# Folding the score rows in two ahead of a top-32 selection, with GpSimd making the smaller halves and VectorE closing the gates

## Chip, cores and metric

One Trainium2 chip, one NeuronCore of it. The time is that of the device from the first to the last instruction of the slowest core (here the only one), in microseconds. The engines are TensorE (PE; PEld is its weight load), VectorE (DVE), ScalarE (ACT), GpSimd (POOL) and SyncE (SP), which issues the DMAs.

## What is computed

Attention that keeps, in each row of scores, only the 32 largest (and what ties with the 32nd), then a feed-forward layer with ELU. Eight batches, eight heads, 576 positions, head size 64; 4608 tokens of 512 go through 512 x 2048 and 2048 x 512 weights.

```python
scores = scale * np.matmul(q, k.transpose(0, 1, 3, 2))
kth = np.partition(scores, -top_k, axis=-1)[..., -top_k:-top_k + 1]   # top_k = 32
scores = np.where(scores >= kth, scores, -1000000000.0)
attn = np.exp(scores - np.max(scores, axis=-1, keepdims=True))
attn = attn / (np.sum(attn, axis=-1, keepdims=True) + 1e-09)
x = ...  # np.matmul(attn, v), heads side by side: 4608 x 512
h = x @ w_in
g = np.where(h > 0.0, h, np.exp(np.minimum(h, 0.0)) - 1.0)
out = g @ w_out
```

The weights arrive as 64-bit floats and are decoded to 32 bits by the kernel's first part.

## The kernel before

**Steps.** A step is one tile of 128 queries for two heads: two rows of 576 scores on each partition. There are 144, eighteen to a batch. The list `steps` fixes their order, and the loop at the end of the function writes the program for step n with work of four ages side by side: scores of step n+2, selection of step n, mask of step n-1 (`prev`), transposes of step n-2 (`done`). From step 8 on (`tight`) the order on PE, ACT, DVE and POOL is the order in which the code writes the instructions; nothing is moved afterwards. Each engine works its own list in that order and waits where an operand is not there.

**One step, in the order written.** `scores` (L331, copied out of PSUM by ACT at L339) for n+2; `attend` (L470) when a group of steps is turned; then the selection `select`, a generator that the loop advances four times, and between the pieces: `feed`; `mask(prev, 0)`; `feed`; `turn(done, main)` and `turn(done, rest)`; `mask(prev, 1)`; `feed`; `turn(done, other)`; `normalise(prev)`; `feed`.

- `select` (DVE): for each of the two rows MAX8 gives the eight largest, MATCH_REPLACE8 (with a load of the eight values) strikes them out, four rounds in all; L373, L378, L385. `u.first` keeps the first eight (the largest is the maximum), `u.last` the last eight (the last is the 32nd largest).
- `mask`: POOL takes the gap of 32nd and largest (L406); ACT makes a steep Prelu about the 32nd (L407), then the Exp with its sum (L408, with the gap as bias).
- `normalise` (POOL): five small operations for the reciprocal (L418 to L423), then each row times it (L425).
- `turn`: nine 128 x 128 transposes on PE (L444), copied to `et` by ACT (L445).
- `attend`: product with v on PE, ACT copies it into the block's `xT` (L497).

**The feed-forward beside it.** Tokens are gathered in blocks of one, two or three slots of 128. When the last head of a block is there, `ffn_pieces` appends its pieces: sixteen of `hidden` (four products each, L545) and four of `project` for each slot (L573). `feed`, four times a step, hands out as many pieces as the costs `HIDDEN` and `PROJECT` and the due times of the blocks allow. A unit of hidden is two pieces or more: ACT writes Relu(-h) to `n` (L555) and Relu(h) to `gT` (L558), then Exp of -n (L560). What is left, gT + n - 1, is the gate. It is put on the list `gates` and written by `close_gates` at a later feed (two feeds later, as a rule), or at the latest when a `project` needs it. Until some way past step 11, and for the last block, the gate is one operation on DVE (L517). For all others ACT first takes 1 from `n` (L564) and POOL adds (L515).

**Early steps.** Steps 0 to 7 select row by row (`select_row`) and share the engines with the decoding of the weights, in 37 pieces run by `hook`, at the end of rounds of the selection. When the list is empty, `hook` opens the pools that take the place of the raw weights (the dictionary `late`).

Of the kernel before, what the change touches and what calls it, by code (L numbers as in the profile page):

```python
# [7 lines left out]

AF = mybir.ActivationFunctionType
ALU = mybir.AluOpType  # L10
FP32 = mybir.dt.float32
U32 = mybir.dt.uint32
I32 = mybir.dt.int32
# [3 lines left out]
TOP_K = 32  # L17
TAKEN = -1.0e30
# [63 lines left out]
def kernel(  # L82
# [9 lines left out]
    nc = tc.nc  # L92
    P = nc.NUM_PARTITIONS
    B, H, S, D = q.shape
# [4 lines left out]
    HS = S // 2  # L99
# [4 lines left out]
    T = 3 * P  # L104
# [7 lines left out]
    def pool(name, bufs, **kw):  # L112
        return ctx.enter_context(tc.tile_pool(name=name, bufs=bufs, **kw))
# [4 lines left out]
    wkpool = pool("wk", 1)  # L118
    etpool = pool("et", 2)
    small = pool("small", 4)  # L120
# [2 lines left out]
    ps_sc = pool("ps_sc", 1, space=PSUM)  # L123
    ps_t = pool("ps_t", 2, space=PSUM)
    ps_f = pool("ps_f", 2, space=PSUM)
    wide = [ps_sc.tile([P, 2, JP], FP32, tag=f"s{i}", name="scps") for i in range(2)]
    late = {}
    raws = ExitStack()
# [70 lines left out]
    def hook():  # L199

        if not decode:
            return
        decode.pop(0)()
        if not decode:
            raws.close()
            late["f"] = ctx.enter_context(tc.tile_pool(name="f", bufs=2))
            late["g"] = ctx.enter_context(tc.tile_pool(name="g", bufs=2))
            late["x"] = ctx.enter_context(tc.tile_pool(name="xt", bufs=2))
            late["in"] = ctx.enter_context(tc.tile_pool(name="in", bufs=2))
# [134 lines left out]
    def select_row(u, i, decoding):  # L344
        if i == 0:
            u.first = small.tile([P, 2, 8], FP32, tag="m1", name="m1")
            u.last = small.tile([P, 2, 8], FP32, tag="m4", name="m4")
        sc = u.sc[:, i, :]
        m = u.first[:, i, :]
        nc.vector.max(m, sc)  # L350
        wk = wkpool.tile([P, S], FP32, tag=f"wk{i}", name="wk")
        cur = sc
        for r in range(TOP_K // 8 - 1):
            nc.vector.match_replace(wk[:], m, cur, TAKEN)
            cur = wk[:]
            if r < TOP_K // 8 - 2:
                m = small.tile([P, 8], FP32, tag=f"m{i}", name="m")[:]
            else:
                m = u.last[:, i, :]
            nc.vector.max(m, cur)  # L360
            if r > 0 and decoding:
                hook()
            if r != 1:
                yield

    def select(u):

        u.first = small.tile([P, 2, 8], FP32, tag="m1", name="m1")
        u.last = small.tile([P, 2, 8], FP32, tag="m4", name="m4")
        cur = [u.sc[:, i, :] for i in range(2)]  # L370
        found = [u.first[:, i, :] for i in range(2)]
        for i in range(2):
            nc.vector.max(found[i], cur[i])  # L373
        yield
        wk = [wkpool.tile([P, S], FP32, tag=f"wk{i}", name="wk")[:] for i in range(2)]
        for r in range(TOP_K // 8 - 1):
            for i in range(2):
                nc.vector.match_replace(wk[i], found[i], cur[i], TAKEN)  # L378
            cur = wk
            for i in range(2):  # L380
                if r < TOP_K // 8 - 2:
                    found[i] = small.tile([P, 8], FP32, tag=f"m{i}", name="m")[:]
                else:
                    found[i] = u.last[:, i, :]
                nc.vector.max(found[i], cur[i])  # L385
            hook()
            yield

    def mask(u, i, early=False):

# [111 lines left out]
    gates = []  # L502
    place = [0]

    def close_gates(keep=0, upto=None):

        while gates:
            put, group, dst, n, apart = gates[0]  # L510
            if put > place[0] - keep if upto is None else group > upto:
                return
            gates.pop(0)
            if apart:
                nc.gpsimd.tensor_tensor(dst, n, dst, ALU.add)  # L515
                continue
            nc.vector.scalar_tensor_tensor(  # L517
                out=dst, in0=n, scalar=-1.0, in1=dst, op0=ALU.add, op1=ALU.add
            )

    def ffn_pieces(blk):
        n_tok = blk.slots * P
        bank = dm // n_tok
        unit = max(2, bank)

        def hidden(f):
            if f == 0 and blk.number == 0:
                g = early.tile([P, NF, P], FP32, tag="g", name="gT")
                blk.gT = [g[:, 0:NG], g[:, NG:NF]]
            elif f % NG == 0 and blk.number > 0:  # L530
                g = late["g"].tile([P, NG, T], FP32, tag="g", name="gT")
                blk.gT.append(g[:])
            if f % unit == 0:
                if len(gates) > 1:
                    close_gates(upto=gates[0][1])
                if blk.number == 0:
                    n = earlyf.tile([P, 4 * P], FP32, tag="n", name="n")
                else:
                    n = late["f"].tile([P, 2 * T], FP32, tag="n", name="n")
                blk.n = n[:, 0 : unit * n_tok].rearrange("p (f t) -> p f t", f=unit)  # L540
            if f % bank == 0:
                ps = ps_f.tile([P, dm], FP32, tag="f", name="hps")
                blk.h = ps[:, 0 : bank * n_tok].rearrange("p (f t) -> p f t", f=bank)
            for i in range(NC):
                nc.tensor.matmul(  # L545
                    blk.h[:, f % bank, :],
                    w_in[:, i, f * P : (f + 1) * P],
                    blk.xT[:, i, 0:n_tok],
                    start=(i == 0),
                    stop=(i == NC - 1),  # L550
                )
            g, end = blk.gT[f // NG], f % NG + 1
            if end % bank == 0:
                n0 = f % unit + 1 - bank
                nc.scalar.activation(  # L555
                    blk.n[:, n0 : n0 + bank, :], blk.h, AF.Relu, scale=-1.0
                )
                nc.scalar.activation(g[:, end - bank : end, 0:n_tok], blk.h, AF.Relu)  # L558
            if end % unit == 0:
                nc.scalar.activation(blk.n, blk.n, AF.Exp, scale=-1.0)  # L560
                dst = g[:, end - unit : end, 0:n_tok]
                apart = place[0] > 4 * (tight + 3) and blk is not blocks[-1]
                if apart:
                    nc.scalar.activation(blk.n, blk.n, AF.Copy, bias=-1.0)  # L564
                gates.append((place[0], (blk.number, f + 1 - unit), dst, blk.n, apart))

        def project(s, part):
            close_gates(upto=(blk.number, (part + 1) * NF // 4 - 1))
            if part == 0:
                blk.o = ps_f.tile([P, dm], FP32, tag="f", name="ops")  # L570
            step = NF // 4
            for f in range(part * step, (part + 1) * step):
                nc.tensor.matmul(  # L573
                    blk.o[:],
                    blk.gT[f // NG][:, f % NG, s * P : (s + 1) * P],
                    w_out[:, f, :],
                    start=(f == 0),
                    stop=(f == NF - 1),
                )
            if part == 3:  # L580
                o = opool.tile([P, dm], FP32, tag="osb", name="osb")
                nc.scalar.copy(o[:], blk.o[:])
                for t in blk.tiles[s]:
                    p0 = t.cols.start - s * P
                    nc.sync.dma_start(out[t.rows, :], o[p0 : p0 + t.ql, :])

        part = HIDDEN[blk.slots]
        behind = 2 * NF if blk.number else 0
        return [
            (part, max(behind, NC * (f // 4 + 1)), lambda f=f: hidden(f))  # L590
            for f in range(NF)
        ] + [
            (PROJECT, max(behind, NF + (part + 1) * NF // 4),
             lambda s=s, part=part: project(s, part))
            for s in range(blk.slots)
            for part in range(4)
        ]
# [3 lines left out]
    blocks, tight = [], 2 * NHP  # L601
    for b in range(B):
        if b % 2 == 0:
            rest = 2 * J
# [4 lines left out]
            for part in division:  # L609
                blk = Block(len(blocks), len(part))  # L610
# [20 lines left out]
        for qts in order:  # L631
            for hp in range(NHP // 2 if qts == (J,) else NHP):
                group = Group([tiles[qt] for qt in qts], hp)
                steps += [Step(tiles[qt], hp, group, i) for i, qt in enumerate(qts)]
            for qt in qts:
                n = len(steps)
# [12 lines left out]
    for b in range(1, B):  # L649
        f = first[b]  # L650
# [51 lines left out]
    for n in range(NS + 3):  # L702
# [24 lines left out]
            continue  # L727
        if n == tight:
            ctx.enter_context(tc.manual_schedule(engines=engines))
        passes = select(cur) if cur else iter(range(4))  # L730
        if ahead and n > tight:
            scores(ahead)
        while closing:
# [58 lines left out]
```

## Time and profile before

| | us |
|---|---|
| median of 3 runs | 1642.47 |
| lowest, highest | 1637.93, 1644.79 |
| profiled execution, span from first to last instruction | 1640.8 |
| PE busy | 1581.7 |
| DVE busy | 1453.4 |
| ACT busy | 1187.7 |
| POOL busy | 708.7 |
| mean granted TensorE clock | 0.974 |

The span is all that the profile gives as the profiled execution's own time; it lies within the three runs. Busy times are sums over the whole span, while the stages differ: up to some 160 us the weights are decoded and the clock is granted in part, and behind 1505 us no selection is left and PE works off the last blocks of the feed-forward. PE's matmuls are pipelined and the ends of them modelled. In the rows of groups, the numbers behind the bar are busy time, the mean of one in ns, and the idle time ahead of them with what ended it.

### The profile page before, as it was taken

The numbers are of one execution on the slowest core, as the hardware profiler recorded it, in microseconds if no ns is written. First come the engines' busy times: TensorE is split into PE (matmuls) and PEld (weight loads), VectorE is DVE, ScalarE is ACT, GpSimd is POOL, SyncE is SP. The second block draws the span as 40 slices with busy tenths as digits, with TensorE's granted clock in tenths as the row PEclk, the third lists the DMA queues.
The fourth block names the chain that finished last, engine by engine and source line by source line (L and its number), as shares of the span: only waits on it lengthen the run. The fifth ranks groups of instructions, "written<-read, shape, count | busy, mean of one in ns | idle before, by whom it ended". The sixth has DMA issues, their size and how long they took to land.

```text
span 1640.8 us, 25344 instructions
## 1 busy us (share of the span) xinstructions
PE 1581.7 (96%) x8276; PEld 1011.8 (62%) x8276; DVE 1453.4 (89%) x2981; ACT 1187.7 (72%) x2400; POOL 708.7 (43%) x1534
## 2 busy tenths in 40 slices
PE   4788999999999999999999999999999999999999
PEld 3566777666575757555566666655557575755564
DVE  6987999999999999999999699999999599998000
ACT  6887778778695867778678686868759595958521
POOL 4775445445353534445335353535435353534300
PEclk8579999999999999999999999999999999999999
DMA  7431221012100310012100211012100201000000
GB/s 226 151 128 25 50 40 26 7 22 45 42 1 7 59 42 8 7 22 44 36 14 15 43 30 28 1 28 44 36 14 0 43 1 35 1 13 2 7 13 14
DMA packets 188037, 56.18 MB, mean 34 GB/s; under 512 B 178177, under 2 KB 179201, under 8 KB 187905
## 3 DMA queue, kind: packets, MB, share of 16 engines
q1 hardware_dynamic: 186704, 54.26, 14.1%
q8 instruction: 66, 1.08, 0.3%
q14 instruction: 67, 0.54, 0.1%
q10 hardware_dynamic: 1200, 0.30, 0.1%
HBM read 45.09 MB, written 9.44 MB: 33 GB/s over the span
## 4 chain that ended last, share of the span: by engine, by line
PE 76%; ACT 12%; DVE 7%; POOL 3%; issue 1%; DMA 1%; SPq 0%; ACTq 0%; DVEq 0%; POOLq 0%
PE ops L573 29%; PE hps L545 23%; PE avps L470 10%; PE scps L331 7%; PE eps L444 6%; DVE wk L378 3%; DVE m L385 3%; ACT sc L408 2%; ACT et L445 2%; ACT sc L407 2%; DVE m L373 1%; ACT n L564 1%; ACT n L555 1%; ACT sc L339 1%; ACT n L560 1%
## 5 line engine op out<-in xcount | busy, mean ns | idle before, releaser
L385 DVE MAX8 m<-wk 128x8 f32<-128x576 f32 x816 | 577.9, 752 | 0.3 <-POOL den L406 0.3
L545 PE MATMUL hps<-xT,w_in 128*128 128x256 f32 (+2 forms) x2432 | 545.8, 374 | 0.0
L573 PE MATMUL ops<-w_out,gT 128*128 128x512 f32 x1152 | 523.6, 599 | 0.0
L545 PEld LDWEIGHTS hps<-xT,w_in 128*128 128x128 f32 x2432 | 406.0, 192 | 100.1 <-issue 26.3
L378 DVE MATCH_REPLACE8 wk<-m,wk 128x576 f32<-128x576 f32 x544 | 401.4, 748 | 0.0
L573 PEld LDWEIGHTS ops<-w_out,gT 128*128 128x128 f32 x1152 | 209.0, 190 | 233.9 <-issue 232.8
L418 POOL TENSOR_SCALAR dene<-den 128x2 f32<-128x2 f32 x144 | 32.9, 228 | 686.5 <-ACT sc L408 686.1
L408 ACT ACTIVATE sc<-sc,den 128x576 f32<-128x576 f32 x288 | 223.6, 776 | 65.5 <-POOL den L406 44.2
L407 ACT ACTIVATE sc<-sc,m 128x576 f32<-128x576 f32 x288 | 225.3, 782 | 10.8 <-DVE m L385 10.7
L470 PE MATMUL avps<-et,vT 128*64 128x256 f32 (+2 forms) x2080 | 207.2, 330 | 17.4 <-ACT et L445 17.2
L425 POOL TENSOR_SCALAR sc<-sc,rec 128x576 f32<-128x576 f32 x288 | 213.0, 750 | 15.0 <-POOL rec L423 0.2
L331 PE MATMUL scps<-kqT 64*128 64x288 f32 (+1 forms) x1280 | 206.0, 442 | 13.6 <-ACT kqT L307 9.1
L339 ACT ACTIVATE sc<-scps 128x576 f32<-128x576 f32 x288 | 171.8, 647 | 65.1 <-PE scps L331 65.1
L445 ACT COPY et<-eps 128x512 f32<-128x512 f32 x288 | 164.6, 571 | 73.4 <-PE eps L444 73.4
L378 DVE MATCH_REPLACE8 wk<-m,sc 128x576 f32<-128x576 f32 x272 | 200.6, 748 | 0.0
L373 DVE MAX8 m<-sc 128x8 f32<-128x576 f32 x272 | 191.6, 749 | 8.8 <-ACT sc L339 8.8
L444 PEld LDWEIGHTS eps<-ident,sc 128*128 128x128 f32 x1152 | 144.9, 144 | 87.2 <-issue 52.7
L444 PE MATMUL eps<-ident,sc 128*128 128x128 f32 x1152 | 177.1, 279 | 13.7 <-POOL sc L425 13.7
L470 PEld LDWEIGHTS avps<-et,vT 128*64 128x64 f32 x2080 | 128.5, 142 | 98.8 <-ACT et L445 31.7
L515 POOL TENSOR_TENSOR gT<-n,gT 128x512 f32<-128x512 f32 (+1 forms) x119 | 164.9, 1386 | 31.2 <-ACT n L564 31.1
L331 PEld LDWEIGHTS scps<-kqT 64*128 64x128 f32 (+1 forms) x1280 | 111.3, 182 | 89.5 <-issue 43.8
L555 ACT ACTIVATE n<-hps 128x512 f32<-128x512 f32 (+1 forms) x156 | 87.3, 559 | 56.8 <-PE hps L545 56.0
(53 smaller groups left out, 1089.6 us busy)
## 6 DMA issues: line engine op xcount, KB each, us to landing
raw<-in_moe_w_in_dram SPq DMA_DIRECT2D x16, 512.0 KB, 6.1
vT<-in_v_dram SPq DMA_DIRECT2D x64, 128.0 KB, 2.5
raw<-in_moe_w_out_dram SPq DMA_DIRECT2D x16, 512.0 KB, 3.6
out_dram<-osb SPq DMA_DIRECT2D x32, 256.0 KB, 2.1
kin<-in_k_dram SPq DMA_DIRECT2D x112, 72.0 KB, 2.5
qin<-in_q_dram SPq DMA_DIRECT2D x112, 72.0 KB, 2.6
kin<-in_k_dram SPq DMA_DIRECT2D x8, 128.0 KB, 4.5
vT<-in_v_dram SPq DMA_DIRECT2D x64, 16.0 KB, 2.2
```

The source lines that it names most:

```text
L331: nc.tensor.matmul(wide[i][rows, half, 0:HS], kq[part, q0 : q0 + u.t.ql], kq[part, k0 : k0 + HS], start=True, stop=True,)
L373: nc.vector.max(found[i], cur[i])
L378: nc.vector.match_replace(wk[i], found[i], cur[i], TAKEN)
L385: nc.vector.max(found[i], cur[i])
L407: nc.scalar.activation(sc, sc, AF.Prelu, scale=-1.0, bias=low, alpha=1.0 / STEEP)
L408: nc.scalar.activation(sc, sc, AF.Exp, scale=-STEEP, bias=gap, accum_out=u.den[:, i : i + 1])
L425: nc.gpsimd.tensor_scalar(u.sc[:, i, :], u.sc[:, i, :], rec[:, i : i + 1], 1.0, ALU.mult, ALU.mult)
L444: nc.tensor.transpose(ps[:, c * P : (c + 1) * P], sc[:, c0 : c0 + P], ident[:])
L445: nc.scalar.copy(g.et[:, chunks, u.at, :], ps[:, 0 : n * P].rearrange("p (c q) -> p c q", c=n),)
L470: nc.tensor.matmul(ps[i * D : (i + 1) * D, cols], vt[:, 2 * J + i if c == J else i * J + c, :], w, start=(c == 0), stop=(c == J),)
L545: nc.tensor.matmul(blk.h[:, f % bank, :], w_in[:, i, f * P : (f + 1) * P], blk.xT[:, i, 0:n_tok], start=(i == 0), stop=(i == NC - 1),)
L573: nc.tensor.matmul(blk.o[:], blk.gT[f // NG][:, f % NG, s * P : (s + 1) * P], w_out[:, f, :], start=(f == 0), stop=(f == NF - 1),)
```

## The change

In steps that begin when `late` is filled, `select_folded` takes the place of `select`. DVE compares the left half of each row (288) with the right half and keeps the larger (`high`). POOL adds the two halves as 32-bit integers and takes `high` away, which leaves the bits of the smaller one (`low`). The four rounds run over `high`; two rounds over `low` give its sixteen largest. The 32nd of the row is the largest of `found[31]` and of the minima of the pairs found[15..30] and second[15..0]; DVE forms it with a minimum and a reduce into `u.last[..., 7]`. The two halves of one work tile `wk`, now opened once at the start, hold `rest` (what is left of `high`) and `low`.

All gates are the one operation on DVE; ACT's subtraction and POOL's addition go. In blocks of three slots a unit is one piece, so that the gate and its Exp are 384 wide instead of 768.

```diff
+    wk = wkpool.tile([P, 2, S], FP32, tag="wk", name="wk")
...
             raws.close()
+            late["high"] = ctx.enter_context(tc.tile_pool(name="high", bufs=1))
+            late["top"] = ctx.enter_context(tc.tile_pool(name="top", bufs=3))
...
+    def select_folded(u):
+        one, other = u.sc[:, :, 0:HS], u.sc[:, :, HS:S]
+        high = late["high"].tile([P, 2, HS], FP32, tag="high", name="high")
+        rest, low = (
+            wk[:, i, :].rearrange("p (a s) -> p a s", a=2) for i in range(2)
+        )
+        found = late["top"].tile([P, 2, TOP_K], FP32, tag="found", name="found")
+        second = late["top"].tile([P, 2, TOP_K // 2], FP32, tag="second", name="second")
+        u.first = found
+        u.last = small.tile([P, 2, 8], FP32, tag="m4", name="m4")
+        nc.vector.tensor_tensor(high[:], one, other, ALU.max)
+        nc.gpsimd.tensor_tensor(
+            low.bitcast(I32), one.bitcast(I32), other.bitcast(I32), ALU.add
+        )
+        nc.gpsimd.tensor_tensor(
+            low.bitcast(I32), low.bitcast(I32), high[:].bitcast(I32), ALU.subtract
+        )
+        for i in range(2):
+            nc.vector.max(found[:, i, 0:8], high[:, i, :])
+        yield
+        cur = high
+        for r in range(0, TOP_K - 8, 8):
+            for i in range(2):
+                nc.vector.match_replace(
+                    rest[:, i, :], found[:, i, r : r + 8], cur[:, i, :], TAKEN
+                )
+            cur = rest
+            for i in range(2):
+                nc.vector.max(found[:, i, r + 8 : r + 16], rest[:, i, :])
+            if r < TOP_K - 16:
+                yield
+        for i in range(2):
+            nc.vector.max(second[:, i, 0:8], low[:, i, :])
+        for i in range(2):
+            nc.vector.match_replace(low[:, i, :], second[:, i, 0:8], low[:, i, :], TAKEN)
+        for i in range(2):
+            nc.vector.max(second[:, i, 8:16], low[:, i, :])
+        pairs = found[:, :, TOP_K // 2 - 1 : TOP_K - 1]
+        nc.vector.tensor_tensor(pairs, pairs, second[:, :, ::-1], ALU.min)
+        nc.vector.tensor_reduce(
+            u.last[:, :, 7:8], found[:, :, TOP_K // 2 - 1 : TOP_K], AX.X, ALU.max
+        )
+        yield
...
-            put, group, dst, n, apart = gates[0]
+            put, group, dst, n = gates[0]
...
-            if apart:
-                nc.gpsimd.tensor_tensor(dst, n, dst, ALU.add)
-                continue
             nc.vector.scalar_tensor_tensor(
...
-        unit = max(2, bank)
+        unit = max(2, bank) if blk.slots < 3 else 1
...
-                apart = place[0] > 4 * (tight + 3) and blk is not blocks[-1]
-                if apart:
-                    nc.scalar.activation(blk.n, blk.n, AF.Copy, bias=-1.0)
-                gates.append((place[0], (blk.number, f + 1 - unit), dst, blk.n, apart))
+                gates.append((place[0], (blk.number, f + 1 - unit), dst, blk.n))
...
-        passes = select(cur) if cur else iter(range(4))
+        choose = select_folded if late else select
+        passes = choose(cur) if cur else iter(range(4))
```

More of the change, by code (lines that the diff above doesn't have):

```diff
@@ L10 @@
 ALU = mybir.AluOpType
+AX = mybir.AxisListType
 FP32 = mybir.dt.float32
@@ L350, in select_row @@
         nc.vector.max(m, sc)
-        wk = wkpool.tile([P, S], FP32, tag=f"wk{i}", name="wk")
         cur = sc
         for r in range(TOP_K // 8 - 1):
-            nc.vector.match_replace(wk[:], m, cur, TAKEN)
-            cur = wk[:]
+            nc.vector.match_replace(wk[:, i, :], m, cur, TAKEN)
+            cur = wk[:, i, :]
             if r < TOP_K // 8 - 2:
@@ L374, in select @@
         yield
-        wk = [wkpool.tile([P, S], FP32, tag=f"wk{i}", name="wk")[:] for i in range(2)]
         for r in range(TOP_K // 8 - 1):
             for i in range(2):
-                nc.vector.match_replace(wk[i], found[i], cur[i], TAKEN)
-            cur = wk
+                nc.vector.match_replace(wk[:, i, :], found[i], cur[i], TAKEN)
+            cur = [wk[:, i, :] for i in range(2)]
             for i in range(2):
@@ L538, in hidden @@
                 else:
-                    n = late["f"].tile([P, 2 * T], FP32, tag="n", name="n")
+                    n = late["f"].tile([P, 4 * P], FP32, tag="n", name="n")
                 blk.n = n[:, 0 : unit * n_tok].rearrange("p (f t) -> p f t", f=unit)
```

## The prediction

> **What bounds the kernel now.** I read the page's busy shares and slices, then the busy time by stretches, then the order of time inside one step, then the groups. The page first: span, busy time by engine, and the 40 slices.
>
> ```profile
> PE 1581.7 (96%) x8276; PEld 1011.8 (62%) x8276; DVE 1453.4 (89%) x2981; ACT 1187.7 (72%) x2400; POOL 708.7 (43%) x1534
> ...
> PE   4788999999999999999999999999999999999999
> ...
> DVE  6987999999999999999999699999999599998000
> ...
> POOL 4775445445353534445335353535435353534300
> ```
>
> PE is nearly full from the fourth slice to the end, DVE until slice 37. The stretches (columns: length, then PE, PEld, DVE, ACT and POOL busy, granted clock, DMA) say which of the two leads:
>
> ```profile
> 100.00:200.00 100.00, 92.39 (x590) 66.41 (x590) 86.78 (x175) 82.72 (x169) 52.26 (x93) 0.91 0.24 54
> 200.00:600.00 400.00, 390.80 (x2364) 263.70 (x2363) 400.00 (x823) 305.91 (x619) 181.72 (x419) 1.00 0.14 27
> ...
> 900.00:1300.00 400.00, 398.69 (x2018) 245.40 (x2019) 365.13 (x751) 293.80 (x593) 171.78 (x392) 1.00 0.13 26
> ```
>
> From 200 to 600 DVE never rests and PE waits 9.2 us: DVE leads. From 900 to 1300 PE waits 1.3 us and DVE rests 35: PE leads. So there is little to win. The change removes no matmul; all of PE's waiting from 100 to 1500 is 7.6 + 9.2 + 2.9 + 1.3 + 0.8 = 22 us (the last three from 600:900, 900:1300 and 1300:1500). What was before 100 is not touched, and behind 1505 PE alone works off the last blocks.
>
> The pace: the first MAX8 of step 15 is at 201.3 us and that of step 55 at 600.2, 9.97 us a step. GpSimd's first instruction of the normalisation (L418) is at 608.0 in step 55 and at 1445.9 in step 135, 10.47 us a step, PE's own pace. By then DVE runs ahead: in step 115 L418 starts 28 us after DVE began that step. GpSimd and ScalarE are far from full, but one step shows a chain through both (timeline of step 56, POOL and ACT, start, length):
>
> ```profile
> 608.04 0.23 POOL L418 TENSOR_SCALAR dene<-den 128x2 f32<-128x2 f32 x1 [6.32 <-ACT sc L408]
> ...
> 610.00 1.48 POOL L425 TENSOR_SCALAR sc<-sc,rec 128x576 f32<-128x576 f32 x2
> ...
> 611.85 0.33 POOL L406 TENSOR_TENSOR den<-m,m 128x1 f32<-128x1 f32 x2
> 612.07 0.78 ACT L408 ACTIVATE sc<-sc,den 128x576 f32<-128x576 f32 x1 [0.76 <-POOL den L406]
> ```
>
> Normalise (3.44 us, 608.04 to 611.48), then the gap (L406), then the first Exp (0.22 behind the gap's start), then copies, the second Prelu and Exp, then the next normalise. Each waits for the one before.
>
> **VectorE, part by part.** A step's 8 MAX8 and 6 replacements with loads come each 0.66 us (loads 0.065 more) behind the one before: 8 x 0.66 + 6 x 0.725 = 9.63, the 9.64 between steps 55 and 56 (600.16, 609.80). After: 12 MAX8 and 8 replacements over 288. No row has that width. Bounds: 0.33 (exactly half) and 0.66 (no gain); I take 0.36, which is 576 elements in 0.60 us halved plus a fixed 0.06. That gives 20 x 0.36 + 8 x 0.065 = 7.72. The fold reads two tensors over 576 like the gate at L517 (0.69 for 512): 0.76, between 0.57 (the one-input L189, 512 wide) and 0.94 (L517's mean of 0.83, for 576). The minimum and the reduce over 16 or 17 elements: 0.3 together (between two loads, 0.16, and two half MAX8, 0.7). Sum 8.8, so 0.85 less a step in steps 11 to 143, 133 of them: the pieces of the weight decoding are 37, 28 go in steps 0 to 6 and three in each of 8, 9, 10, and only then is `late` filled. Saved: 113 us.
>
> The gates come back: 95 x 0.69, and the 24 gates of 768 become 48 of 384, 0.56 each by the same slope: 66 + 27 = 93 us. Net DVE gains 20 us in 1453, before it meets GpSimd. Its step is then 8.8 + 0.65 for gates + 0.31 for transposes (42.3 us by 136) = 9.8. **No real relief.**
>
> **ScalarE.** L564 goes: 59.9 + 20.2 = 80 us, 0.6 a step; the 24 Exps of 768 (0.85) become 48 of 384 (0.49, as L555 at that width): +3. ACT is at 72%, so this counts only inside the chain above.
>
> **GpSimd.** It loses 119 gates, 165 us, and gets 2 x 133 integer sums over 576. The nearest rows:
>
> ```profile
> L515 POOL TENSOR_TENSOR gT<-n,gT x119: 1262/1277/1829, 175.0 to 1538.4; 128x512 f32<-128x512 f32 x95, 128x768 f32<-128x768 f32 x24
> L517 DVE SCALAR_TENSOR_TENSOR gT<-n,gT x13: 684/693/1625, 102.8 to 1611.1; 128x512 f32<-128x512 f32 x13
> L193 POOL TENSOR_TENSOR w_in<-w_in,raw x16: 1277/1292/1474, 11.1 to 85.2; 128x512 int32<-128x512 int32 x16
> ```
>
> Int32 at 512 is 1.29; the float rows grow by 2.1 ns an element; so 1.29 + 64 x 0.0021 = 1.43 each, 2.86 both, 2.95 with the 0.09 that dependent instructions of this engine stand apart (L420 to L421). Bounds: 1.5 (two at L425's 0.75) and 3.6 (both stretched as L193's 1.757). +390 - 165: POOL ends near 930 us, 57%, which looks harmless. **Its place is not.** The sums stand at the head of step n, behind normalise(n-2) and ahead of both gaps of n-1, and the Exps wait for those. The second sum also waits for `high`, but DVE makes that early. So the chain becomes normalise 3.44 + sums 2.95 + gap 0.22 + from the first Exp to the next normalise 3.23 (604.80 to 608.04) = 9.84 us. In 44 of 136 steps (counted in ACT's order of time) the piece of the second feed puts two Relus and an Exp between the Exps (5.38 before with the Copy at L564, so 4.75 after): 11.36. Mean 9.84 + 0.32 x 1.52 = 10.33, plus 0.07 for vT's memsets (9.3 us over 136) and 0.04 for nine pairs of output copies: **10.44**. Before it was 7 to 9. And DVE's lead goes: its second half now needs this step's sums, so it can no longer stand three steps in front.
>
> Queued behind the sums on POOL: both gaps, memsets, normalise. PE waits for normalise (eps, L444), DVE for the sums and, at its gates, for ScalarE's Exp, which DVE did not do before; with the gates kept back two feeds I cost those waits at nothing, DVE having 10.44 - 9.8 = 0.6 us a step to spare. SP's queue and its DMAs are not moved.
>
> **The sum.** Steps 12 to 55 are paced at 9.97; at 10.44 they lose 43 x 0.47 = 20 us. The other 88 go at 10.47 anyway, but the 11.36 steps come four in a row (steps 78 to 81, 86 to 89, and so on), 4 x 0.9 = 3.6 us behind PE in each run. The chain can stand ahead of PE by 10.47 less what must follow PE's transposes (transposes and copies 1.6, Prelu and Exp 1.8, normalise 3.4), 3.7 us, if the steps before let it. I take half lost, 1.8 x 8 runs (six of four, the pairs of 41 to 60 counted as two) = 15. Ports, below: 5. The span is 1640.8; I add 40: **1680 us**. The shown runs have a median of 1642.47, 1.7 above the span, far below what I can resolve.
>
> **Two engines at one port.** Of the gates DVE made while POOL ran large operations, three took 1.20, 1.63 and 1.08 us against 0.69 alone, and ended about 0.55 behind POOL's instruction; POOL's took 1.757 and 1.164 there against 1.29 and 0.75. The one-input MAX8 beside POOL is 0.75 throughout. From these rows: 276 new two-input operations (133 folds, 143 gates), if one in five adds 0.4 on either engine, are 22 us of engine time, of which I put a quarter in the chain: 5; the upper end is 0.4 in every step, 53.
>
> The Trainium skill ("SBUF — State Buffer", SBUF: two separate sides) says the pair of ports that VectorE and GpSimd share is an exclusive lock held for a whole instruction, taken by a VectorE operation with two SBUF inputs. The rows above agree. By it alone each fold that meets a sum waits up to 1.4 us; at every fold that would be 133 x 0.7, an estimate of 93 us on DVE instead of my few. The same skill ("GPSIMD Engine Reference", Elementwise — side-by-side cycle accounting) has 2.6 cycles an element for GpSimd's two-input sums, which speaks against putting them there; the row's 2.1 ns an element is the same.
>
> **Rivals.**
> 1. *The chain keeps inside its slack* (within 0.5%, 1633 to 1649). For: base waits are small, ACT loses 0.6 a step, and PE leads from 600 on. Against: stage 200 to 600 has 9.97. It needs the sums at about 2.5.
> 2. *Faster, the other side*: DVE was what PE waited for from 100 to 600, and 0.2 less DVE a step plus a lighter ACT lets PE go without a wait. Place: steps 11 to 55. Price: the 7.6 + 9.2 us there, up to 22 in all: 1619 to 1632. It decides once the pair of sums costs under 2.95 - 0.47 = 2.5 us, as it would nearer L425's row than L193's.
> 3. *Two prices higher*: halves at 0.42 instead of 0.36 make DVE's step 11.0 with gates; or ports add 0.4 to the chain; or the two halves of `wk` are held as one, so that DVE's replacements wait for the sums. At 10.9 a step: 43 x 0.9 + 88 x 0.4 = 74, 1715; at 11.3: 57 + 73 = 130, 1770.
> 4. *It doesn't do what it says*: the fold starts late or not at all. By the count of pieces above it starts at step 11; I give it nothing.
>
> **Numbers.** Forecast case (1650 to 1705): 0.44. Rival 1: 0.18. Rival 2: 0.20. Rival 3: 0.18. Half a per cent, 8 us, is about what a measurement of this kernel can tell from no change; so faster 0.20, same 0.18, slower 0.62. The range takes in rival 1 and most of 2 and 3: 1625 to 1750.
>
> **What would show it.** Right: L418's starts 10.4 us or more apart in 200 to 600; PE's waits for POOL sc (13.7 us) and ACT et (17) growing to some 50; sums of 1.43; DVE resting, mostly for the sums; ACT's Exps waiting for den (44 us before) by far more. Wrong: PE still full from 200 to 1500, the sums under 1.25, or DVE full at over 10 us a step.

## The result, and the profile after

The changed kernel takes 1727.57 us (median; 1726.9 to 1728.18), the kernel before beside it 1641.8: a ratio of 1.0518, interval 1.05 to 1.0536. The forecast was slower, 1680 in 1625 to 1750. The sign and the mechanism held; the size was off by half (86 us measured, 40 forecast), and nearly the whole miss, 42 of 47 us, is in one term of the sum, the one for the shared port.

First the page of the changed kernel: span, busy time by engine, the 40 slices of PE, DVE and POOL, and the shares of the chain that ended last.

```profile
span 1725.1 us, 27135 instructions
...
PE 1628.8 (94%) x8276; PEld 1029.4 (60%) x8276; DVE 1456.8 (84%) x4587; ACT 1099.1 (64%) x2305; POOL 970.3 (56%) x1681
...
PE   5789999999999999999999999999999999999999
...
DVE  6978999998998998998988998889988898887600
...
POOL 3765666665656566555655655556665556555400
...
PE 30%; POOL 28%; ACT 21%; DVE 14%; issue 5%; DMA 1%; SPq 0%; POOLq 0%; DVEq 0%; ACTq 0%
```

Read alone, the first lines mislead. PE looks as full as before, no other engine is full, and POOL at 56% seems to have room. Only the last line speaks. Before, PE's share of the chain was 76% and POOL's 3%:

```profile
PE 76%; ACT 12%; DVE 7%; POOL 3%; issue 1%; DMA 1%; SPq 0%; ACTq 0%; DVEq 0%; POOLq 0%
```

Now POOL has 28 and ACT 21. PE's busy time grew by 47 us with the same 8276 matmuls. Their own durations, added up, grew by only 23 us in 3227; busy time counts matmuls that overlap once, so the rest is that fewer of them overlap. Here are the stretches, with the columns as before (length, then PE, PEld, DVE, ACT and POOL busy, clock, DMA):

```profile
200.00:600.00 400.00, 376.73 (x2156) 252.06 (x2156) 365.57 (x1199) 255.50 (x535) 243.72 (x423) 0.98 0.13 26
...
900.00:1300.00 400.00, 390.30 (x1936) 239.67 (x1933) 360.54 (x1175) 259.43 (x550) 235.64 (x417) 1.00 0.12 25
```

Nobody is full in either: PE has fewer matmuls in the same 400 us (2156 instead of 2364), and DVE, which never rested there, now rests 34. The loss by steps, from the starts of the normalisations of steps 15, 55, 95 and 135:

| stretch | before, us | after, us | more | a step, before and after |
|---|---|---|---|---|
| start to step 15 | 218.8 | 224.4 | 5.6 | |
| 15 to 55 | 398.1 | 432.5 | 34.4 | 9.95, 10.81 |
| 55 to 95 | 420.1 | 444.1 | 24.0 | 10.50, 11.10 |
| 95 to 135 | 419.9 | 441.8 | 21.9 | 10.50, 11.05 |
| 135 to the end | 183.9 | 182.3 | -1.6 | |

It is spread over all steps up to 135. One round shows what sets the pace. First POOL, then ACT, then one line of DVE, in the order of time (start, length; in brackets idle time ahead and what ended it).

```profile
1112.74 0.23 POOL L465 TENSOR_SCALAR dene<-den 128x2 f32<-128x2 f32 x1 [4.62 <-ACT sc L455]
...
1114.71 1.98 POOL L472 TENSOR_SCALAR sc<-sc,rec 128x576 f32<-128x576 f32 x2
1116.66 1.40 POOL L403 TENSOR_TENSOR wk<-sc 128x576 int32<-128x576 int32 x1
1118.14 1.41 POOL L406 TENSOR_TENSOR wk<-wk,high 128x576 int32<-128x576 int32 x1
1119.51 0.33 POOL L453 TENSOR_TENSOR den<-m,found 128x1 f32<-128x1 f32 x2
1124.46 0.23 POOL L465 TENSOR_SCALAR dene<-den 128x2 f32<-128x2 f32 x1 [4.62 <-ACT sc L455]
```

```profile
1119.73 0.78 ACT L455 ACTIVATE sc<-sc,den 128x576 f32<-128x576 f32 x1 [3.09 <-POOL den L453]
...
1123.50 0.78 ACT L455 ACTIVATE sc<-sc,den 128x576 f32<-128x576 f32 x1
```

```profile
1114.65 0.69 DVE L561 SCALAR_TENSOR_TENSOR gT<-n,gT 128x512 f32<-128x512 f32 x1 [0.25 <-ACT n L604]
```

Normalise begins at 1112.74; the two sums follow at once; the gap; the first Exp, for which ACT had waited 3.09 us; the second Exp; and the next normalise at 1124.46, 11.72 later. The mean is 11.0; here two Relus and an Exp of the feed-forward stand between the two Exps, and the two products of normalise take 1.98 instead of 1.48, with a gate of DVE beside the first of them (the last line; run 5 tries this). No part of this round waits for anything outside POOL and ACT. It is a closed loop of the two, and PE and DVE rest because of it. The list of waits has its mark (us in all, times, longest): ACT's Exps waiting for the gap, before and now.

```profile
ACT sc L408 <- POOL den L406: 44.2, 49, 4.3
```

```profile
ACT sc L455 <- POOL den L453: 337.1, 106, 5.4
```

### The profile page after: what moved, and what is told of

It reads as the page before. It is cut to its first block, busy times and chain, and to the rows that moved or that the text cites. A ratio compares the mean times of both kernels' runs of the same rounds, so it can differ in the third digit from the quotient of the medians.

```text
span 1725.1 us, 27135 instructions
## 1 busy us (share of the span) xinstructions
PE 1628.8 (94%) x8276; PEld 1029.4 (60%) x8276; DVE 1456.8 (84%) x4587; ACT 1099.1 (64%) x2305; POOL 970.3 (56%) x1681
## 4 chain that ended last, share of the span: by engine, by line
PE 30%; POOL 28%; ACT 21%; DVE 14%; issue 5%; DMA 1%; SPq 0%; POOLq 0%; DVEq 0%; ACTq 0%
PE ops L614 15%; POOL sc L472 7%; ACT sc L455 6%; POOL wk L406 6%; POOL wk L403 6%; PE hps L589 6%; PE avps L517 5%; ACT sc L454 4%; ACT et L492 4%; POOL rec L467 3%; DVE wk L415 3%; PE scps L335 2%; DVE found L420 2%; DVE second L424 2%; PE eps L491 2%
## 5 line engine op out<-in xcount | busy, mean ns | idle before, releaser
L420 DVE MAX8 found<-wk 128x8 f32<-128x288 f32 x798 | 323.1, 446 | 0.0
L335 PE MATMUL scps<-kqT 64*128 64x288 f32 (+1 forms) x1280 | 226.3, 444 | 35.9 <-ACT et L492 23.3
L517 PE MATMUL avps<-et,vT 128*64 128x256 f32 (+2 forms) x2080 | 228.3, 337 | 30.8 <-ACT et L492 30.1
L472 POOL TENSOR_SCALAR sc<-sc,rec 128x576 f32<-128x576 f32 x288 | 233.6, 821 | 14.9 <-POOL rec L470 0.2
L415 DVE MATCH_REPLACE8 wk<-found,wk 128x288 f32<-128x288 f32 x532 | 231.2, 442 | 0.0
L561 DVE SCALAR_TENSOR_TENSOR gT<-n,gT 128x512 f32<-128x512 f32 (+1 forms) x156 | 112.5, 721 | 113.1 <-ACT n L604 113.1
L406 POOL TENSOR_TENSOR wk<-wk,high 128x576 int32<-128x576 int32 x133 | 190.7, 1434 | 10.4
L335 PEld LDWEIGHTS scps<-kqT 64*128 64x128 f32 (+1 forms) x1280 | 118.8, 182 | 124.9 <-issue 44.8
L491 PE MATMUL eps<-ident,sc 128*128 128x128 f32 x1152 | 177.5, 280 | 15.2 <-POOL sc L472 15.1
L403 POOL TENSOR_TENSOR wk<-sc 128x576 int32<-128x576 int32 x133 | 190.7, 1434 | 0.0
L424 DVE MAX8 second<-wk 128x8 f32<-128x288 f32 x266 | 108.3, 448 | 89.0 <-POOL wk L406 88.9
L492 ACT COPY et<-eps 128x512 f32<-128x512 f32 x288 | 164.8, 572 | 23.7 <-PE eps L491 23.7
```

What stands on the lines that cost most here:

```text
L335: nc.tensor.matmul(wide[i][rows, half, 0:HS], kq[part, q0 : q0 + u.t.ql], kq[part, k0 : k0 + HS], start=True, stop=True,)
L403: nc.gpsimd.tensor_tensor(low.bitcast(I32), one.bitcast(I32), other.bitcast(I32), ALU.add)
L406: nc.gpsimd.tensor_tensor(low.bitcast(I32), low.bitcast(I32), high[:].bitcast(I32), ALU.subtract)
L415: nc.vector.match_replace(rest[:, i, :], found[:, i, r : r + 8], cur[:, i, :], TAKEN)
L420: nc.vector.max(found[:, i, r + 8 : r + 16], rest[:, i, :])
L472: nc.gpsimd.tensor_scalar(u.sc[:, i, :], u.sc[:, i, :], rec[:, i : i + 1], 1.0, ALU.mult, ALU.mult)
```

## Experiments

The theory (the *ring*): normalise, sums, gap, Exps, next normalise bound every step. Its rivals: *ports* (VectorE's new two-input operations and GpSimd delay each other wherever they stand) and *VectorE* (it has become the bound by folds, gates and their waits). The expectations call the ring the "chain theory". From run 5 on, "collision theory" says that what the ring has beyond the forecast comes from GpSimd's instructions that are stretched, inside the ring, beside VectorE's operations with two inputs. All ratios are to the kernel before, run on the same chip; a difference of two runs in us can be one of two chips.

**1. Gaps ahead of the sums.**

```diff
+        if prev and not prev.masked:
+            gaps(prev)              # the two POOL subtractions, out of mask()
         next(passes)                # fold and sums of this step
```

> The changed kernel, but the two gaps of the step before are written ahead of the sums on GpSimd; nothing is left out. Chain theory (normalise, sums, gap, Exp, next normalise in one ring of 11.0 us a step): the sums leave the ring, which falls to about 11.0 - 3.0 = 8.0 us, below TensorE's 10.4 to 10.5; time 1630 to 1655, as before the change or a little under it. Port rival (the new two-input operations on VectorE and GpSimd delay each other, whatever the order): the collisions stay, at least half of the loss stays, 1685 or more. VectorE rival (gates and folds fill VectorE, which waits for ScalarE's Exp): unchanged near 1725.

Measured: 1638.24 us, 0.9968 (0.9955 to 0.9981). Moving two operations of 0.2 us takes back the whole loss and a little more: no sum is less, no gate is less, only the place has changed. The steps run at 10.06, 10.38 and 10.44 us. The two rivals, as the main cause, fall. The collisions did not go: GpSimd's normalise, sums and gaps were stretched by 87 us in this run, more than the 56 of the changed kernel, and VectorE's gates, folds and minima by 51 instead of 15. Outside the ring they leave the kernel no slower than before; what VectorE's still cost is the question of runs 9 and 10.

**2. The smaller halves on VectorE.**

```diff
-        nc.gpsimd.tensor_tensor(low.bitcast(I32), one.bitcast(I32), other.bitcast(I32), ALU.add)
-        nc.gpsimd.tensor_tensor(low.bitcast(I32), low.bitcast(I32), high[:].bitcast(I32), ALU.subtract)
+        nc.vector.tensor_tensor(low, one, other, ALU.min)
```

> The changed kernel, but the smaller halves are one minimum on VectorE; GpSimd makes no sums; nothing is left out. Chain theory: the ring falls to about 8, and VectorE becomes the longest: 8.9 for the selection as measured after, 0.7 for the minimum, 0.65 for gates, 0.31 for transposes, 10.55 a step; 43 early steps lose 0.6 each against before (26 us), the other 88 some 0.1 (9 us): 1665 to 1685. Port rival: half of the collisions go (no sums to hit), the folds and gates still meet normalise; 1700. VectorE rival: 0.7 us more a step on VectorE, 1725 + 90 = 1815.

Measured: 1662.49, 1.0117 (1.0102 to 1.0132), just under the ring's span of times. With the sums gone the ring is, too (ACT's Exps wait 18.7 us for the gap), and VectorE leads (397 of 400 us in both long stretches).

**3. The gates alone**, on the kernel before: the `apart` branch and ScalarE's subtraction go, one piece to a unit in three-slot blocks.

> The kernel before with the gates part of the change alone (all gates on VectorE, one piece to a unit in three-slot blocks); nothing is left out. Chain theory: no sums, so the ring is short; VectorE at 9.64 + 0.65 + 0.31 = 10.6 a step leads: 27 us in the early steps and 11 later, 1670 to 1690. Port rival: gates meet normalise in GpSimd only, some 20 us, 1660. VectorE rival: the gates' waits for ScalarE are the loss, 1700 or more.

Measured: 1663.71, 1.0125 (1.011 to 1.014), 6 us under the ring's span and nearer to the port rival's number, but the profile says which it was. Its stretches:

```profile
200.00:600.00 400.00, 382.90 (x2244) 259.21 (x2241) 400.00 (x814) 272.75 (x558) 138.86 (x360) 0.98 0.14 27
...
900.00:1300.00 400.00, 397.09 (x2020) 245.71 (x2016) 400.00 (x818) 278.32 (x574) 138.99 (x361) 1.00 0.12 25
```

VectorE never rests, and GpSimd waits 214 us for it at the gap, so that its own stretching (26 us) had room. A step takes 10.48 us in the early stretch, 0.53 more than before, and 10.51 to 10.55 later, as before. So the gates part costs 20 us by itself.

**4. The fold alone**: the changed kernel with ScalarE's subtraction and GpSimd's additions put back (but still one-piece units in three-slot blocks).

> The changed kernel with the gates as before (ScalarE subtracts, GpSimd adds); nothing is left out. Chain theory: half of the gates' additions lie between normalise and gap, 0.88 x 1.28 x 0.5 = 0.56 us a step, and the subtraction of 0.6 in a third of the steps 0.2, less some 0.2 of collisions: the ring is 11.5, 1780 to 1810. Port rival: 143 two-input operations fewer on VectorE, 1700 or less. VectorE rival: 0.65 us a step less on VectorE, 1650.

Measured: 1793.78, 1.092 (1.0902 to 1.0938). Undoing half of the change makes it worse by 66 us, and inside the span that the ring gave: the additions now lie between normalise and gap. Part of the 66 belongs to the three-slot blocks (runs 6 and 12).

**5. The gates' last operation left out**, so that `gT` lacks the Exp's branch and the -1.

```diff
             gates.pop(0)
-            nc.vector.scalar_tensor_tensor(
-                out=dst, in0=n, scalar=-1.0, in1=dst, op0=ALU.add, op1=ALU.add
-            )
```

> The changed kernel with the gates' last operation left out (the Exp's branch and the -1 never reach gT, so the feed-forward lacks them); all else as changed. Collision theory: GpSimd's normalise, sums and gaps were stretched by 56 us in all beside VectorE's two-input operations, most of it by gates, and that time stood in the ring; without gates the ring is about 10.6 instead of 11.0, 1670 to 1690. Coupling rival (the ring's excess over 10.44 comes from ScalarE and TensorE waiting for one another, the collisions lie beside): 1715 to 1727.

Measured: 1680.94, 1.0229 (1.0214 to 1.0244): 47 us less than the changed kernel, as the collision theory expected. The row that carries it is normalise's large product; first the changed kernel, then this one (columns behind the bar: busy, mean ns of one, idle ahead).

```profile
L472 POOL TENSOR_SCALAR sc<-sc,rec 128x576 f32<-128x576 f32 x288 | 233.6, 821 | 14.9 <-POOL rec L470 0.2
```

```profile
L472 POOL TENSOR_SCALAR sc<-sc,rec 128x576 f32<-128x576 f32 x288 | 213.0, 750 | 15.0 <-POOL rec L470 0.2
```

750 ns is what it took before the change as well:

```profile
L425 POOL TENSOR_SCALAR sc<-sc,rec 128x576 f32<-128x576 f32 x288 | 213.0, 750 | 15.0 <-POOL rec L423 0.2
```

Summed over normalise, in the changed kernel 107 instructions were stretched, 44 us in all, and every one of them lay beside a VectorE operation with two inputs. They stood in 71 of 132 steps. The median normalise was 3.44 us in this run and 3.68 to 3.89, by stretch, in the changed kernel. Leaving out the gates takes work and waits from VectorE as well, so the ring's terms decide (means, steps 15 to 134): it fell from 10.99 to 10.62 us, normalise by 0.33 and the sums by 0.05, while the two terms through ScalarE stayed (0.44 and 0.46, 3.77 and 3.77). The coupling rival falls.

**6. Gaps first, gates back to ScalarE and GpSimd.** Runs 1 and 4 together.

> Gaps ahead of the sums and the gates as before the change (ScalarE subtracts, GpSimd adds); nothing is left out. Collision theory and chain theory: VectorE has 8.9 + 0.3 = 9.2 us a step, GpSimd 7.9, the ring some 8.5; TensorE leads in the early steps too, 1625 to 1635, under the gaps-first kernel's 1638. Rival (GpSimd's load itself, 66% of the time, is what costs): slower than the gaps-first kernel, 1645 or more.

Measured: 1661.16, 1.0109 (1.0092 to 1.0126). A miss: I had 1625 to 1635. The early steps went at 9.84 us, the best of all to then; the loss stood in three places, steps 64 to 71 (85.4 us against 79.9 before), 100 to 107 (83.9 against 78.9) and 135 to 143 (111.1 against 102.1). They are the three-slot blocks. Run 12 follows this up.

**7. The gap on ScalarE**, sums where they were: `mask(prev, 0, True)` and `mask(prev, 1, True)`.

> The changed kernel with the gap made by ScalarE, as in the early steps, two operations of 0.3 us a step; the sums stay where they are; nothing is left out. Chain theory: the Exps no longer wait for GpSimd, the ring is broken as by the gaps-first order: 1632 to 1645. Rival (the sums hold up normalise and so TensorE's transposes, whatever the gap does): 1690 or more.

Measured: 1723.7, 1.0495 (1.0474 to 1.0516). Also a miss of the chain theory, and the most instructive one; the time is one that the rival allowed. The ring was broken: Exps began a median 2.2 us *ahead* of the end of the sums. Yet nothing was won, and not for the rival's reason either: 70% of the chain that ended last is VectorE, and GpSimd 3%. VectorE's fold, in this kernel (least, median and greatest ns):

```profile
L402 DVE TENSOR_TENSOR high<-sc x133: 710/1740/1968, 154.5 to 1607.1; 128x576 f32<-128x576 f32 x133
...
  POOL wk L406: 118.9, 118
```

The fold's median is 1.74 us; in the changed kernel it was 0.75. POOL now reaches the addition early and waits there for VectorE's last use of the smaller halves (191 us of waiting); so the addition starts just as VectorE comes to the gate and the fold, and one of them stands until it is through. The subtraction then waits for the fold (the second line). Folds (78 us) and gates (60) together cost VectorE 1.0 us a step, and it was full (395 of 400 us in both long stretches): a new bound in place of the old, of the same size by chance.

**8. The addition twice**, into the same place.

> The changed kernel with the integer addition written twice into the same place; nothing is left out. Chain theory: 1.43 us more in a ring that bounds every step from 11 to about 140: +1.43 x 131 = 187, 1900 to 1920. Rival (the loss of the changed kernel comes from several near-equal bounds, of which the ring is one): there is some slack left, +140 or less, 1870 or less.

Measured: 1884.94, 1.1473 (1.1452 to 1.1495), between the two: 157 us, 1.2 of the added 1.43 (with the pause behind it 1.47) in each of 131 steps. Pace 12.13, 12.31 and 12.32. So the ring binds nearly throughout; of the missing 0.2 to 0.3, some 0.1 are collisions that fell (normalise 3.70 instead of 3.78) and 0.1 are the first Exp's own lateness (0.31 instead of 0.44 behind the sums), which the longer sums covered.

**9. Run 1 with the sums in the other order**: left minus larger, then plus right.

```diff
-            low.bitcast(I32), one.bitcast(I32), other.bitcast(I32), ALU.add
+            low.bitcast(I32), one.bitcast(I32), high[:].bitcast(I32), ALU.subtract
...
-            low.bitcast(I32), low.bitcast(I32), high[:].bitcast(I32), ALU.subtract
+            low.bitcast(I32), low.bitcast(I32), other.bitcast(I32), ALU.add
```

> The gaps-first kernel with GpSimd's two sums in the other order (left minus larger, then plus right), so that the first of them needs VectorE's fold and cannot start beside it or beside the gate ahead of it; nothing is left out. Collision theory: VectorE's gates were 35 us longer there than alone and led the early steps (VectorE 396 of 400 us); that time moves from the gates ahead of the fold to those after it, where the sums now stand: 1630 to 1640. Rival (collisions on VectorE cost nothing, TensorE leads): 1638, the same.

Measured: 1639.65, 0.9986 (0.9974 to 0.9998). Run 1's 1638 again; both theories allowed it, so it settles nothing. VectorE's operations with two inputs were stretched as much as in run 1 (54 us against 51; the gates alone 41 against 38).

**10. The same, gates only at the third and fourth feed.**

```diff
-        close_gates(2 if n < tight - 1 or n > tight + 1 else 6)
+        if not late or place[0] % 4 in (3, 0):
+            close_gates(2 if n < tight - 1 or n > tight + 1 else 6)
```

> The same, and gates written at the third and fourth feed of a step only, clear of the sums; nothing is left out. Collision theory: VectorE's two-input operations are at most 15 us longer than alone, early steps go at TensorE's own pace: 1628 to 1636. Rival (later gates hold up TensorE's projections or ScalarE's buffers): 1640 or more.

Measured: 1630.8, 0.9933 (0.9916 to 0.9949), the lowest median of all, though its interval overlaps that of run 12. The time came where it was expected (9.88 us a step early, against 10.08), the reason only in part: the stretching of VectorE's operations with two inputs fell from 54 to 36 us, not below 15. What else the later gates relieve stays open.

**11. Run 7 with the sums in the other order**, so that the first sum needs the fold and cannot start ahead of it.

> The kernel with the gap on ScalarE, and the sums in the other order; nothing is left out. In the gap-on-ScalarE kernel the ring through GpSimd was broken (Exps 2.2 us ahead of the sums' end) but VectorE became full: its folds were 77 us and its gates some 55 us longer than alone, since the addition waits for the last use of the smaller halves and so starts just as the gate and the fold do. Collision theory: with the subtraction first, waiting for the fold, most of those 130 us go; 1640 to 1665. Rival (VectorE is full by its own work and by ScalarE's waits): 1710 or more.

Measured: 1644.62, 1.0015 (1.0004 to 1.0026), 79 us under run 7 by exchanging two operations. The fold again:

```profile
L402 DVE TENSOR_TENSOR high<-sc x133: 709/750/1226, 155.8 to 1531.5; 128x576 f32<-128x576 f32 x133
```

The folds' stretching fell from 78 to 5 us, the gates' from 60 to 43. This shows run 7's loss to be the collision: same work, same engines, another order at the port.

**12. Run 6 with the three-slot blocks' gates on VectorE.**

```diff
-                apart = place[0] > 4 * (tight + 3) and blk is not blocks[-1]
+                apart = place[0] > 4 * (tight + 3) and blk is not blocks[-1] and blk.slots < 3
```

> The kernel with gaps first and gates back, but in the three-slot blocks, whose units are one piece of 384, the gates stay on VectorE (no subtraction on ScalarE, no addition on GpSimd); nothing is left out. In that kernel the early steps went at 9.84 us, faster than any other, and the loss against the kernel before stood in three stretches, those of the three-slot blocks. Theory of the ring: there the one-piece units double the subtractions and additions that lie in the ring, 5 to 9 us in each of the three stretches, and they go: 1632 to 1645. Rival (GpSimd's load as a whole costs): 1655 or more.

Measured: 1633.02, 0.9951 (0.9934 to 0.9967). The three places fell to 76.5, 75.9 and 101.5 us. So what run 6 lost were one-piece units with their subtractions and additions, twice as many as pairs would need, and not GpSimd's load: POOL is as busy in 200 to 600 as in run 6 (308 us), and PE rests only 7.7 there.

## Why the prediction was right in its mechanism and wrong in its size

- *What bounds*: right. PE was within 22 us of full, so there was little to win; the best variant won 11.
- *VectorE*: right. Forecast 0.36 us for an instruction of 288; they come 0.365 apart. The fold 0.75 (0.76 forecast). Its busy time was 1456.8, against 1453.4, where some 20 less was forecast: 15 of the difference are its own stretched operations, most of them gates.
- *GpSimd's sums*: right. 1.43 us each, as worked out; 2.9 the pair (group rows of the changed kernel: busy, mean ns of one, idle ahead).

```profile
L406 POOL TENSOR_TENSOR wk<-wk,high 128x576 int32<-128x576 int32 x133 | 190.7, 1434 | 10.4
...
L403 POOL TENSOR_TENSOR wk<-sc 128x576 int32<-128x576 int32 x133 | 190.7, 1434 | 0.0
```

- *The ring*: right in kind and in most of its terms. Forecast and measured, over steps 15 to 134:

| term | forecast | measured |
|---|---|---|
| normalise | 3.44 | 3.78 |
| sums, with what displaces their start | 2.95 + 0.07 for memsets | 3.00 |
| end of sums to first Exp | 0.22 | 0.44 |
| first Exp to next normalise | 3.23 + 0.32 x 1.52 + 0.04 = 3.76 | 3.77 |
| ring | 10.44 | 10.99 |

- *Ports*: this is the step that failed, "if one in five adds 0.4 on either engine, are 22 us of engine time, of which I put a quarter in the chain: 5". Measured: 47 us (run 5). The 0.4 was right: the 107 stretched instructions of normalise lost 0.41 each. Both shares were wrong. Instructions of normalise, sums and gaps were stretched 137 times, one for every two of the 276 new operations and not for every five: 56 us, not 22. And not a quarter of it but 47 of 56 us counted, since these instructions are the ring. I treated the meetings as chance. They are not: VectorE's second half waits for the sums, then come minimum, reduce, the gates of the fourth feed and the fold, always in that order, and a gate in that row brings VectorE's two-input operations to the time when GpSimd stands in normalise (in run 5, with folds but no gates, 5 instructions were stretched in all). With each gate counted to the normalise nearest to it (steps 12 to 141), 62 of the 78 normalises with a gate were stretched and 9 of the 52 without. The upper end that I gave, "0.4 in every step, 53", lies near the sum but not for its reason: it was 0.6 us in 71 of 132 steps. Without the gates (run 5) the kernel stands 37 us above that of before, beside it; the forecast without its term for ports was 35.
- *First Exp 0.2 later than the gap*: the smaller part. The median is 0.18, near the forecast, but in some rounds ScalarE comes to the Exp up to 4 us after the sums. It does wait for PE at its copies and Relus (62 us at L544, 48 at L599, 24 at L492); that these waits are what makes it late is argued, not tried. I had let only one of the two be late at a time. It is there without the gates too (0.46 in run 5), so it is no part of the 47.
- *DVE loses its lead*: right; it waits 89 us for the sums (L424 on L406). Its waits for ScalarE's Exp at the gates, which I put at nothing, are longer: 113 us in 59 waits, 44 of them in one wait, against 98 in 11 waits before, 67 in one. With the gates left out (run 5) the ring's terms through ScalarE did not move, so no cost of them shows.
- *PE's waits* for ACT et and POOL sc: forecast to grow to some 50, measured 68, but nearly all of it on ACT et (19 us before, 53 after); those for POOL sc only went from 13.7 to 15.1.
- *Rival 3* at its cheaper end (10.9 a step, 1715) was the nearest to the truth, by its port clause. The clause on the halves of `wk` was wrong: in the step shown above, VectorE replaces in the one half at 1117.33 while GpSimd's addition (1116.66 to 1118.06) writes the other.
- *The lock*: the page of the Trainium skill ("SBUF — State Buffer", SBUF: two separate sides), by itself, gave an estimate of 93 us on VectorE for the folds. The folds of the changed kernel were stretched by 0.7 us in all, GpSimd's instructions by 56: VectorE mostly came first. In run 7, where GpSimd came first, the folds lost 78. The lock that the page describes fits both; who pays is set by the order.

## What to carry to other kernels

An engine at 43% can still have no room: look for the closed loop that runs through it, and put new work on an engine where no other engine waits for what is queued behind it. Here two operations of 0.2 us, ahead of 2.9 us of sums instead of behind, were worth 89 us. And where two engines share a port, don't price their meetings by chance; in a kernel with a fixed order they fall into step, and an exchange of two operations can be worth 79 us. They cost time only on what sets the pace: run 1 had more of them than the changed kernel and was no slower than the kernel before.

## What the runs showed of the hardware

- A VectorE operation with two inputs and a large GpSimd operation hardly run side by side: the fold is 0.75 alone and 1.74 (median of run 7) behind an addition of 1.41 us; of 91 such overlaps in the changed kernel (over 0.15 us, with a product or a sum of GpSimd), 87 lengthened one of the two by most of the overlap. GpSimd's instructions of 0.2 us become up to 0.79 beside a fold of 0.75. MAX8 and the replacements beside GpSimd kept their 0.45 and 0.44 throughout.
- The two slowest kernels had the lowest granted clock: 0.945 in run 8 and 0.955 in run 4, against 0.974 before. After 160 us, the kernel before was granted half speed in one spell of 3.4 us, the changed one in six (24 us together), that of run 8 in 27 (133 us), that of run 12 in none; PE's rests over the span (span less busy time) were 59, 96, 176 and 53 us. Whether the rests bring the spells was not tried.
